# An attention kernel of two layers: a fourth score bank at times, its exponentials on VectorE

## Chip, cores, metric

One core of a Trainium2 chip. The metric is device microseconds of one execution. Quoted times are medians; a ratio is the mean time of one kernel's fast runs over the mean of the other's fast runs of the same rounds on the same chip, so it is not quite the ratio of the two medians. Intervals are 95%.

## The reference, cut

```python
def _A_ref(x, wqkv, wo):                      # 16 heads of 28, S = 2048, D = 448
    q, k, v = ...                             # from x @ wqkv
    scores = jnp.einsum("bhqd,bhkd->bhqk", q, k) * scale
    p = _softmax(scores, axis=-1)
    return merge_heads(jnp.einsum("bhqk,bhkd->bhqd", p, v)) @ wo
def _B_ref(x, w1, b1, w2, b2):                # F = 1792, squared ReLU
    ...
x = x + _A_ref(_layernorm(x), A_wqkv, A_wo)   # attention
x = x + _B_ref(_layernorm(x), B_w1, ...)      # FFN
# and both once more, with the same weights
```

## The kernel before

It is a program that plans itself. Streams of operations (scores, exponentials, attention sums, FFN chains, filler) are put in order at build time by a planner that knows a duration for each; every engine is then given its instructions in that order. The kernel divides PSUM (the memory that its matmuls write their sums to) into two score tiles of three banks each (`R_sc`), and a pool of two single banks (`R_m`) that attention outputs, FFN and QKV tiles, transposes and filler share. A bank in this text is what the code calls `bank`: a tile of 128 x 512 fp32. Filler means matmuls whose result nobody reads.

```python
R_sc, R_m, R_pt = Res(2), (Res(1), Res(1)), Res(NPT)
# scores: three units of [128, 512] per group; one unit = one head, 256 queries (or 128), so many keys
groups = [units[i:i + 3] for i in range(0, len(units), 3)]
def s_stream():
    for gi, us in enumerate(groups):
        ...                                   # 32-row matmuls, one row tile per head
        o = Op("PE", 0.22 + 0.01 * mm, fn, deps=list(deps), acq=R_sc, mode="row", sets=("s", gi), need=1 + cut)
def e_stream():                               # ScalarE: one exponential per group
    ...
    nc.scalar.activation(out=pt[:, 0:n], in_=gbuf[gi]["sc"][:, 0:n], func=AF.Exp,
                         scale=float(np.log(2.0)) * 2.0 ** -23)
# ... p_stream: sums over keys, an output bank of the pool held from the first to the last
# the filler: keeps TensorE's load up, takes a pool bank
def heat():
    for gi in range(1, len(groups)):
        yield Op("-", 0.0, None, deps=[("s", gi)])
        short = 0.74 - pl.load(WINDOW)        # planned load of the last 2.8 us
        if short <= 0 or not s_left:
            continue
        k = 1 if short < 0.14 else 2
        def junk(e):
            t = bank(o, "mt")
            for _ in range(k):
                nc.tensor.matmul(t[:, 0:D], lhsT=ident[:, :], rhs=xns[0][:, 0:D], start=True, stop=True)
        o = Op("PE", 0.19 * k, junk, deps=[("s", gi)], acq=R_m)
        ...
```

The scores come scaled by 2^23 times log2 e, so that an exponential can also be had on VectorE: add the exponent bias and convert to an integer (`take`), mask out the mantissa and the exponent field, three steps of a polynomial in the mantissa, and one that multiplies by the power of two. This code is in the kernel before (it would take the third bank of a score tile), but `LAST = 0` switches it off.

The softmax here doesn't subtract the row's maximum and nothing guards it: scores larger than these inputs give would overflow.

## Time and profile before

| | before |
|---|---|
| median of runs | 961.8 us |
| span of the profiled run | 957.4 us |
| ScalarE, TensorE, VectorE busy | 97%, 88%, 46% |
| exponentials on ScalarE | 683 (2048 units) |
| filler matmuls on TensorE | 345, 104 us |
| ScalarE's idle time before exponentials | 1.7 us |
| last exponential ends, tail after it | 936.0 us, 21.4 us |

A row of the groups gives the line, the engine, the output and inputs with shapes, the count, then busy time and mean duration, then how long the engine sat idle before these instructions and who ended that. A row of the stretches gives the busy time of TensorE, its weight loads, VectorE, ScalarE and GpSimd, then the granted TensorE clock (1.00 is full), the DMA share and GB/s. The lines of the kernel before are in the prediction.

### The profile page before, as it was taken

What the parts mean: (1) busy time and instruction counts of PE and PEld (TensorE: products, weight loads), DVE (VectorE), ACT (ScalarE), POOL (GpSimd) and SP (SyncE); (2) the same over time, 40 slices, a digit from 0 to 9 for tenths busy, and PEclk for the clock granted to TensorE, in tenths of its full rate; (3) what the DMA queues carried; (4) which work ended last, traced back from release to release, by engine and by line L of the source; (5) the groups of instructions that cost most, each with busy time, mean ns of one, the idle gap of its engine ahead of it and who ended that gap; (6) DMA issues with size and microseconds to landing.
All of it is one profiled execution on the core that took longest, in us unless ns stands there. A gap on an engine that the chain in (4) does not pass through costs nothing.

```text
span 957.4 us, 27259 instructions
## 1 busy us (share of the span) xinstructions
PE 838.9 (88%) x12123; PEld 431.9 (45%) x12123; DVE 443.1 (46%) x1151; ACT 928.7 (97%) x700; POOL 7.6 (1%) x16
## 2 busy tenths in 40 slices
PE   8999779898989898998989977779899989788886
PEld 4555334444444444444444433334444434455654
DVE  7855244555364544636464411144734434153444
ACT  6999999999999999999999999999999999999992
POOL 3000000000000000000000000000000000000000
PEclk9999999999999999999999999999999999999999
DMA  9000010000000000000000000011000000000000
GB/s 276 4 2 2 8 41 9 13 13 8 13 13 7 14 13 8 13 14 1 1 2 2 1 2 1 11 35 35 18 23 17 15 21 12 21 12 21 19 11 11
DMA packets 34467, 18.31 MB, mean 19 GB/s; under 512 B 18475, under 2 KB 33900, under 8 KB 34349
## 3 DMA queue, kind: packets, MB, share of 16 engines
q1 hardware_dynamic: 34348, 16.58, 6.2%
q8 instruction: 94, 1.54, 0.7%
q14 instruction: 25, 0.20, 0.1%
HBM read 14.26 MB, written 2.07 MB: 17 GB/s over the span
## 4 chain that ended last, share of the span: by engine, by line
ACT 76%; issue 16%; PE 6%; DVE 1%; DMA 0%; ACTq 0%
ACT pt L633 76%; PE mt L467 2%; PE sc L614 1%; PE sc L467 1%; PE mt L909 1%; PE oT L736 1%; DVE st L357 0%; DMA x_sb<-in_A_x_dram 0%; PE tp L409 0%; DVE xn L434 0%; DVE x_sb L833 0%; ACT Q_sb L482 0%; DVE tt L385 0%; DVE rstd L390 0%; DVE ve L380 0%
## 5 line engine op out<-in xcount | busy, mean ns | idle before, releaser
L633 ACT ACTIVATE pt<-sc 128x1536 bf16<-128x1536 f32 (+1 forms) x683 | 917.8, 1831 | 1.7 <-PE sc L614 1.6
L614 PE MATMUL sc<-Q_sb,K_sb 32*128 32x256 bf16 (+1 forms) x4608 | 270.5, 259 | 93.4 <-ACT pt L633 88.9
L614 PEld LDWEIGHTS <-K_sb 32*128 32x128 bf16 x4608 | 108.8, 92 | 277.5 <-issue 268.1
L736 PE MATMUL oT<-pt,V_sb 128*32 128x256 bf16 (+1 forms) x4608 | 153.8, 263 | 0.3 <-DVE K_sb L761 0.3
L467 PE MATMUL mt<-xnT,w 128*128 128x256 bf16 (+1 forms) x952 | 123.5, 266 | 6.4 <-DVE r L864 2.2
L864 DVE TENSOR_SCALAR r<-mt 128x512 bf16<-128x512 f32 (+1 forms) x109 | 74.4, 683 | 87.1 <-PE mt L467 86.6
L736 PEld LDWEIGHTS <-V_sb 128*32 128x32 bf16 x4608 | 93.0, 96 | 45.6 <-issue 41.3
L909 PE MATMUL mt<-xn,ident 128*128 128x448 bf16 x345 | 104.2, 358 | 2.4 <-DVE x_sb L833 0.7
L467 PE MATMUL mt<-w,h 128*128 128x448 bf16 x434 | 102.1, 355 | 1.5 <-DVE x_sb L833 1.2
L467 PEld LDWEIGHTS <-w 128*128 128x128 bf16 x1008 | 81.4, 99 | 43.9 <-issue 32.7
L833 DVE TENSOR_TENSOR x_sb<-x_sb,mt 128x448 bf16<-128x448 bf16 x62 | 38.2, 616 | 101.2 <-PE mt L467 101.0
L467 PEld LDWEIGHTS <-h 128*128 128x128 bf16 x448 | 34.9, 97 | 43.8 <-issue 22.3
L868 DVE TENSOR_TENSOR h<-r 128x512 bf16<-128x512 bf16 x114 | 47.7, 419 | 8.0 <-ACT r L862 4.8
L761 DVE COPY oT_sb<-oT 128x256 f32<-128x256 f32 (+1 forms) x52 | 19.7, 380 | 65.4 <-PE oT L736 64.9
L909 PEld LDWEIGHTS <-ident 128*128 128x128 bf16 x345 | 25.0, 97 | 37.8 <-issue 31.9
L357 DVE BATCH_NORM_STATS2 st<-x_sb 128x6 f32<-128x448 bf16 x64 | 39.8, 622 | 2.0 <-DMA x_sb<-in_A_x_dram 0.7
L467 PE MATMUL mt<-xnT,wk 128*128 128x256 bf16 x256 | 36.1, 276 | 2.4 <-DVE xnT L419 2.2
L822 DVE TENSOR_TENSOR oTn<-oT_sb,rec 128x256 bf16<-128x256 f32 (+1 forms) x72 | 27.7, 386 | 20.5 <-DMA rec<-scr 20.3
L467 PE MATMUL mt<-xnT,wq 128*128 128x256 bf16 x240 | 33.8, 274 | 0.6 <-DVE K_sb L488 0.5
L488 DVE CAST K_sb<-mt 128x512 bf16<-128x512 f32 x30 | 20.7, 690 | 28.3 <-PE mt L467 28.1
L763 DVE TENSOR_TENSOR K_sb<-oT,K_sb 128x256 f32<-128x256 f32 x28 | 11.9, 424 | 45.9 <-PE oT L736 45.6
L484 DVE TENSOR_SCALAR Q_sb<-mt 128x512 bf16<-128x512 f32 x30 | 20.7, 690 | 24.6 <-PE mt L467 23.4
(71 smaller groups left out, 386.6 us busy)
## 6 DMA issues: line engine op xcount, KB each, us to landing
rec<-scr SPq DMA_DIRECT2D x52, 128.0 KB
x_sb<-in_A_x_dram SPq DMA_DIRECT2D x8, 224.0 KB
out_dram<-x_sb SPq DMA_DIRECT2D x16, 112.0 KB
w<-in_B_w_dram SPq DMA_DIRECT2D x1, 1568.0 KB
w<-in_B_w_dram SPq DMA_DIRECT2D x1, 1344.0 KB
dn<-oT_sb SPq DMA_DIRECT2D x52, 4.0 KB
scr<-dn SPq DMA_DIRECT2D x52, 4.0 KB
rec<-scr SPq DMA_DIRECT2D x12, 64.0 KB
```

Of the source, the lines that this page charges most:

```text
L357: nc.vector.bn_stats(out=st[:, :], in_=x_sb[:, t0 + j, :])
L467: nc.tensor.matmul(box["t"][:, c0:c0 + n], lhsT=lhsT() if callable(lhsT) else lhsT, rhs=rhs, start=a, stop=b)
L484: nc.vector.tensor_scalar(out=dst, in0=src, scalar1=by, scalar2=None, op0=ALU.mult)
L488: nc.vector.tensor_copy(out=dst, in_=src)
L614: nc.tensor.matmul(sc[:, c0:c0 + nt * P], lhsT=K_sb[l][rows, g, (kb + i) * P:(kb + i + 1) * P], rhs=Q_sb[rows, g, t0 * P:(t0 + nt) * P], s ...
L633: nc.scalar.activation(out=pt[:, 0:n], in_=gbuf[gi]["sc"][:, 0:n], func=AF.Exp, scale=float(np.log(2.0)) * 2.0 ** -23)
L736: nc.tensor.matmul(box["t"][DHP * hh:DHP * hh + DHP, 0:n], lhsT=V_sb[l][:, kb + i, 4 * g + hh, :], rhs=p[:, c0:c0 + n], start=begin and kb ...
L822: nc.vector.tensor_tensor(out=oTn_of[l, qb][0][:, g, 0:n], in0=res["t"][:, 0:n], in1=box["r"][:, 0:n], op=ALU.mult)
L833: nc.vector.tensor_tensor(out=x_sb[:, tb, :], in0=x_sb[:, tb, :], in1=t[:, 0:D], op=ALU.add)
L864: nc.vector.tensor_scalar(out=r[:, 0:w], in0=t[:, 0:w], scalar1=0.0, scalar2=None, op0=ALU.max)
L868: nc.vector.tensor_tensor(out=h[:, 0:w], in0=r[:, 0:w], in1=r[:, 0:w], op=ALU.mult)
L909: nc.tensor.matmul(t[:, 0:D], lhsT=ident[:, :], rhs=xns[0][:, 0:D], start=True, stop=True)
```

## The change

The intent: ScalarE, the bound, gives some units to VectorE, which is idle half the time (46% busy), without shortening ScalarE's instructions. A group may get a fourth unit, whose scores go to a bank of the shared pool. Conditions are tested at each group; filler and transposes now yield the last free bank. `NEAR`, `FAR` and `LAG` were counted in groups of three units and are now counted in units, so 9 and 15 are the old 3 and 5.

```diff
-NEAR = 3
-FAR = 5
+NEAR = 9
+FAR = 15
-LAG = 5
+LAG = 6
-LAST = 0
+LAST = 690
 ...
-            if s_left and p_next[0] is not None and e_now[0] >= p_next[0] - (NEAR if n < 8 else FAR):
+            if s_left and (want[0] or p_next[0] is not None and e_now[0] >= p_next[0] - (NEAR if n < 8 else FAR)):
                 return R_m if all(r.when() is not None for r in R_m) else ()
 ...                                           # transposes of the layer norm:
-            t = Op("PE", ..., acq=pools_now(early))
+            t = Op("PE", ..., acq=pools_now(early) if early else spare(1))
 ...
+    def apart(i, now):
+        want[0] = False
+        if not LEAD <= len(gbuf) <= LAST or i + LAG > ends_at[units[i][0]]:
+            return False                       # the last six units of a pass are barred
+        if aside[0] is not None and (aside[0].end is None or aside[0].end > now):
+            return False                       # one at a time
+        if any(... keys or queries not there ...):
+            return False
+        if pl.load(SPAN, "DVE") > BUSY:
+            return False
+        near = p_next[0] is not None and e_now[0] >= p_next[0] - NEAR
+        want[0] = sum(r.when() is not None and r.when() <= now for r in R_m) < 1 + near
+        return not want[0]                     # a pool bank must be free
 ...                                           # in s_stream:
+                if at[0] < len(units) and apart(at[0], o.start):
+                    us = us + [units[at[0]]]
+                    ...
+                    dst.append(bank(x, "mt"))
+                    pl.spawn(C_PRIO, a_first(gi, x, dst[-1]))
 ...                                           # the filler:
-            o = Op("PE", 0.19 * k, junk, deps=[("s", gi)], acq=R_m)
+            o = Op("PE", 0.19 * k, junk, deps=[("s", gi)], acq=spare(1))
```

Cut: the bookkeeping by which the attention sums find the unit in the group (`where`, `done`, `got`), and the steps on VectorE, which are as before except for their source.

More of the change, by code (lines that the diff above doesn't have):

```diff
@@ L1 @@
+import itertools
 from contextlib import ExitStack
@@ L341 @@
     p_next = [None]
-    e_now = [0]
+    e_now = [0, 0]
+    want = [False]
     def engs_now(early=False):
@@ L410, in tr @@
                                             in_=xn[:, dc * P:(dc + 1) * P], identity=ident[:, :])
-            t = Op("PE", 0.07 * NDC * len(xs), tr, deps=[x[1] for x in xs], acq=pools_now(early))
+            t = Op("PE", 0.07 * NDC * len(xs), tr, deps=[x[1] for x in xs],
+                   acq=pools_now(early) if early else spare(1))
             yield t
@@ L573 @@
                 units.append((pi, kb, r, hh))
-    groups = [units[i:i + 3] for i in range(0, len(units), 3)]
-    gbuf = [{} for _ in groups]
-    ends_at = {}
-    for gi, us in enumerate(groups):
-        for pi, *_ in us:
-            ends_at[pi] = gi
-    aside = {}
-    def apart(gi):
-        us = groups[gi]
-        if len(us) < 3 or gi < LEAD or gi > LAST or gi + LAG > ends_at[us[-1][0]]:
+    ends_at = {pi: i for i, (pi, *_) in enumerate(units)}
+    gbuf = []
+    where = {}
+    at = [0]
@@ L586, in apart @@
+    aside = [None]
+    def apart(i, now):
+        want[0] = False
+        if not LEAD <= len(gbuf) <= LAST or i + LAG > ends_at[units[i][0]]:
             return False
-        if any(end is None for end in aside.values()) or pl.load(SPAN, "DVE") > BUSY:
+        if aside[0] is not None and (aside[0].end is None or aside[0].end > now):
             return False
-        aside[gi] = None
-        return True
-    def s_stream():
-        for gi, us in enumerate(groups):
-            deps = set()
-            mm = 0
-            cut = apart(gi)
-            for pi, kb, r, hh in us:
-                l, qb, g, *_ = passes[pi]
-                t0, nt = blocks[l][qb]
-                deps |= {("K", l, g, kb + i) for i in range(r)}
-                deps |= {("Q", l, g, t0 + i) for i in range(nt)}
-                mm = max(mm, r)
-            def fn(e, gi=gi, us=us):
-                sc = gbuf[gi]["sc"] = ps_sc.tile([P, 3 * 512], DT.float32, name="sc", tag="sc")
+        if any(pl.tok.get(d) is None or pl.tok[d].end + LAT["DVE"] > now for d in needs(units[i])):
+            return False
[4 more added lines that the diff above has]
+        return not want[0]
@@ new lines, in needs @@
+    def needs(unit):
+        pi, kb, r, hh = unit
+        l, qb, g, *_ = passes[pi]
+        t0, nt = blocks[l][qb]
+        return [("K", l, g, kb + i) for i in range(r)] + [("Q", l, g, t0 + i) for i in range(nt)]
+    def s_stream():
+        while at[0] < len(units):
+            gi = len(gbuf)
+            us = units[at[0]:at[0] + 3]
+            gbuf.append({"n": len(us)})
+            def fn(e, gi=gi, us=us):
+                sc = ps_sc.tile([P, 3 * 512], DT.float32, name="sc", tag="sc")
+                gbuf[gi]["sc"] = sc
+                dst = [sc[:, k * 512:k * 512 + 512] for k in range(len(us))]
+                at[0] += len(us)
+                if at[0] < len(units) and apart(at[0], o.start):
+                    us = us + [units[at[0]]]
+                    at[0] += 1
+                    x = aside[0] = gbuf[gi]["x"] = Op("PE", 0.0, None)
+                    x.res = min((r for r in R_m if r.when() is not None), key=lambda r: r.when())
+                    x.turn = len(x.res.rel)
+                    x.res.rel.append(None)
+                    dst.append(bank(x, "mt"))
+                    pl.spawn(C_PRIO, a_first(gi, x, dst[-1]))
+                for k, (pi, kb, r, hh) in enumerate(us):
+                    where.setdefault((pi, kb), []).append((gi, k, hh))
+                    if len(where[pi, kb]) == G:
+                        pl.tok["u", pi, kb] = o
@@ L612, in fn @@
                         rows = slice(DHP * hh, DHP * hh + DHP)
-                        c0 = k * 512 + i * nt * P
-                        nc.tensor.matmul(sc[:, c0:c0 + nt * P],
+                        nc.tensor.matmul(dst[k][:, i * nt * P:(i + 1) * nt * P],
                                          lhsT=K_sb[l][rows, g, (kb + i) * P:(kb + i + 1) * P],
@@ L617, in fn @@
                                          start=True, stop=True, tile_position=(DHP * hh, 0))
-            o = gbuf[gi]["s"] = Op("PE", 0.22 + 0.01 * mm, fn, deps=list(deps), acq=R_sc, mode="row",
-                                   sets=("s", gi), need=1 + cut)
-            if cut:
-                pl.spawn(C_PRIO, a_first(gi))
+            o = gbuf[gi]["s"] = Op("PE", 0.22 + 0.01 * max(u[2] for u in us), fn,
+                                   deps=list({d for u in us for d in needs(u)}), acq=R_sc, mode="row", sets=("s", gi))
             yield o
@@ L625, in e_stream @@
     def e_stream():
-        for gi, us in enumerate(groups):
+        gi = 0
+        while gi < len(gbuf) or s_left:
             yield Op("-", 0.0, None, deps=[("s", gi)])
-            n = (len(us) - (gi in aside)) * 512
+            n = gbuf[gi]["n"] * 512
             def fn(e, gi=gi, n=n):
-                e_now[0] = gi
+                e_now[:] = [e_now[0] + n // 512 + ("x" in gbuf[gi]), gi]
                 pt = gbuf[gi]["pt"] = ptp.tile([P, 3 * 512], DT.bfloat16, name="pt")
@@ L634, in fn, with a_first @@
                                      scale=float(np.log(2.0)) * 2.0 ** -23)
-            o = gbuf[gi]["e"] = Op("ACT", n / 1200 + 0.068, fn, deps=[("s", gi)], acq=R_pt, need=len(us) - (gi in aside),
+            o = gbuf[gi]["e"] = Op("ACT", n / 1200 + 0.068, fn, deps=[("s", gi)], acq=R_pt, need=n // 512,
                                    rel=gbuf[gi]["s"], sets=("e", gi))
             yield o
-    def a_first(gi):
+            gi += 1
+    def a_first(gi, x, src):
         yield Op("-", 0.0, None, deps=[("s", gi)])
@@ L644, in take @@
             box["i"] = vp.tile([P, 512], DT.int32, name="vi")
-            nc.vector.tensor_scalar(out=box["i"][:, :], in0=gbuf[gi]["sc"][:, 1024:1536], scalar1=EXP_BIAS,
+            nc.vector.tensor_scalar(out=box["i"][:, :], in0=src, scalar1=EXP_BIAS,
                                     scalar2=0.0, op0=ALU.add, op1=ALU.max)
-        c = Op("DVE", 0.70, take, acq=R_v, rel=gbuf[gi]["s"], sets=("y", gi))
+        c = Op("DVE", 0.70, take, deps=[("s", gi)], acq=R_v, rel=x)
         yield c
@@ L679, in a_rest @@
         o = Op("DVE", 0.68, close, deps=[o], acq=R_pd, rel=c, sets=("x", gi))
-        aside[gi] = gbuf[gi]["x"] = o
+        aside[0] = gbuf[gi]["x"] = o
         yield o
@@ L686, in p_stream @@
     def p_stream():
-        steps = [{} for _ in passes]
-        last_use = {}
-        for gi, us in enumerate(groups):
-            for k, (pi, kb, r, hh) in enumerate(us):
-                steps[pi].setdefault(kb, []).append((gi, k, hh))
-                last_use[gi] = pi, kb
         for pi, (l, qb, g, kbs, first, last) in enumerate(passes):
@@ L697, in p_stream @@
             r, n = 4 // nt, nt * P
-            todo = list(steps[pi].items())
+            todo = list(kbs[::r])
             end = pi == len(passes) - 1
             some = 1 if end else CHUNK
-            hold = 0 if end else max(gi for gi, _, _ in todo[min(HOLD * len(todo) // 8, len(todo) - 1)][1])
+            hold = todo[0 if end else min(HOLD * len(todo) // 8, len(todo) - 1)]
             box = {}
-            p_next[0] = hold
-            def there(parts):
-                return all(("x", gi) in pl.tok if k == 2 and gi in aside else ("e", gi) in pl.tok for gi, k, _ in parts)
@@ L707, in p_stream, with done, got @@
-            yield Op("-", 0.0, None, deps=[("e", hold)])
+            p_next[0] = next(i for i, u in enumerate(units) if u[0] == pi and u[1] == hold) + G - 1
+            def done(kb):
+                return ("u", pi, kb) in pl.tok and all(("x" if k == 3 else "e", gi) in pl.tok for gi, k, _ in where[pi, kb])
+            def got(kb):
+                yield Op("-", 0.0, None, deps=[("u", pi, kb)])
+                yield Op("-", 0.0, None, deps=[("e", gi) for gi, k, _ in where[pi, kb] if k < 3])
@@ L708, in p_stream @@
+            yield from got(hold)
             while todo:
-                now = [t for t in todo if there(t[1])][:some]
+                now = [kb for kb in todo if done(kb)][:some]
                 if len(now) < min(some, len(todo)):
-                    missing = next(t for t in todo if not there(t[1]))[1]
-                    if ("e", missing[-1][0]) not in pl.tok:
-                        yield Op("-", 0.0, None, deps=[("e", missing[-1][0])])
+                    kb = next(kb for kb in todo if not done(kb))
+                    if ("u", pi, kb) not in pl.tok or any(k < 3 and ("e", gi) not in pl.tok for gi, k, _ in where[pi, kb]):
+                        yield from got(kb)
@@ L714, in p_stream @@
                         continue
-                    if e_now[0] - missing[0][0] < NPT - KEEP and e_now[0] < len(groups) - 1 and len(todo) > len(now) + 1:
-                        yield Op("-", 0.0, None, deps=[("e", e_now[0] + 1)])
+                    if (e_now[1] - min(gi for gi, _, _ in where[pi, kb]) < NPT - KEEP and e_now[1] < len(gbuf) - 1
+                            and len(todo) > len(now) + 1):
+                        yield Op("-", 0.0, None, deps=[("e", e_now[1] + 1)])
                         continue
-                    now = [t for t in todo if there(t[1]) or t[1] is missing][:some]
@@ L720, in p_stream @@
-                    if not any(t[1] is missing for t in now):
-                        now[-1] = next(t for t in todo if t[1] is missing)
-                    yield Op("-", 0.0, None, deps=[("x", gi) for gi, k, _ in missing if k == 2 and gi in aside])
-                todo = [t for t in todo if t not in now]
+                    now = sorted(now[:some - 1] + [kb])
+                    yield Op("-", 0.0, None, deps=[("x", gi) for gi, k, _ in where[pi, kb] if k == 3])
+                todo = [kb for kb in todo if kb not in now]
@@ L724, in p_stream, with fn @@
                 begin, close = "t" not in box, not todo
-                def fn(e, now=now, begin=begin, close=close, box=box, l=l, g=g, r=r, n=n):
+                def fn(e, now=now, begin=begin, close=close, box=box, pi=pi, l=l, g=g, r=r, n=n):
                     if "t" not in box:
@@ L729, in fn @@
                         box["t"] = bank(box["o"], "oT")
-                    for kb, parts in now:
+                    for kb in now:
                         for i in range(r):
-                            for gi, k, hh in parts:
+                            for gi, k, hh in where[pi, kb]:
                                 p, c0 = gbuf[gi]["pt"], k * 512 + i * n
-                                if k == 2 and gi in aside:
+                                if k == 3:
                                     p, c0 = gbuf[gi]["pd"], i * n
@@ L738, in fn @@
                                                  rhs=p[:, c0:c0 + n],
-                                                 start=begin and kb == now[0][0] and i == 0,
-                                                 stop=close and kb == now[-1][0] and i == r - 1,
+                                                 start=begin and kb == now[0] and i == 0,
+                                                 stop=close and kb == now[-1] and i == r - 1,
                                                  tile_position=(0, DHP * hh))
-                gis = [gi for _, parts in now for gi, k, _ in parts if not (k == 2 and gi in aside)]
-                xs = [gi for _, parts in now for gi, k, _ in parts if k == 2 and gi in aside]
+                by = [(("x" if k == 3 else "e"), gi) for kb in now for gi, k, _ in where[pi, kb]]
                 o = Op("PE", 0.02 + 0.22 * len(now), fn,
-                       deps=[("e", max(hold, *gis)), *{("V", l, kb + i) for kb, _ in now for i in range(r)},
-                             *[("x", gi) for gi in xs]],
+                       deps=[*by, *{("V", l, kb + i) for kb in now for i in range(r)}],
                        acq=None if "o" in box else pools_now(),
-                       rel=[gbuf[gi]["e"] for gi in gis] + [gbuf[gi]["x"] for gi in xs], mode="col")
+                       rel=[gbuf[gi][w] for w, gi in by], mode="col")
                 box.setdefault("o", o)
@@ L896, in heat @@
     def heat():
-        for gi in range(1, len(groups)):
+        for gi in itertools.count(1):
+            if not s_left:
+                return
             yield Op("-", 0.0, None, deps=[("s", gi)])
```

## The prediction

Terms are cut from it: rules of the hardware that no trace of this case showed, and with them the price of the two masks and the four fused steps on VectorE. The sum came to 4.30 us of VectorE per unit, 4.7 with gaps between the steps. Of it only the first step, 690 ns, was a measured row; the 3.95 of the cycle and the 4.3 of the load limit come from the rest of that sum, so the count of 72 rests on the estimate. The 0.448 us per unit that ScalarE saves does not. What the trace of the kernel before shows on VectorE: 690 ns for a step of 512 columns out of PSUM, 424 ns for one on two bf16 tensors of 512 columns, 416 ns for one on two fp32 tensors of 256. The row tile is an estimate from the numbers beside it; in that trace the first three matmuls of a score group, of 32 rows each, begin within 10 ns of one another and take 278 ns each in the median.

> **What bounds the kernel now.** I read the shares of busy time first, then the chain that ended last, then the cost groups and the waits, and last the stretches of time, because what the change needs is spread unevenly over the span. From the page:
>
> ```profile
> span 957.4 us, 27259 instructions
> PE 838.9 (88%) x12123; PEld 431.9 (45%) x12123; DVE 443.1 (46%) x1151; ACT 928.7 (97%) x700; POOL 7.6 (1%) x16
> ACT 76%; issue 16%; PE 6%; DVE 1%; DMA 0%; ACTq 0%
> ```
>
> ScalarE is busy 97% of the span and carries the chain; VectorE is busy less than half. The groups by form and the waits say what ScalarE does and that nobody starves it:
>
> ```profile
> L633 ACT ACTIVATE pt<-sc 128x1536 bf16<-128x1536 f32 x682 | 916.9, 1832 | 1.7 <-PE sc L614 1.6
> ...
> L909 PE MATMUL mt<-xn,ident 128*128 128x448 bf16 x345 | 104.2, 358 | 2.4 <-DVE x_sb L833 0.7 <-DVE r L864 0.7 <-DVE xn L434 0.6
> ```
>
> ```profile
> PE sc L614 <- ACT pt L633: 88.9, 181, 0.9
> ...
> ACT pt L633 <- PE sc L614: 1.6, 3, 0.6
> ```
>
> The 2048 score units (one head, 512 scores per partition, one PSUM bank) are exponentiated three at a time. ScalarE waited 1.6 us in all for scores, TensorE 88.9 us for ScalarE to free a score tile. The mean of 1832 ns is not the pace, since neighbours overlap: 916.9/682 = 1.344 us per exponential of 1536 columns, so **0.448 us per unit**. TensorE's 88% is partly filler: the 345 matmuls with the identity (104.2 us) are junk that keeps its load up. Real work is 838.9 - 104.2 = 735 us, 77% of the span.
>
> By stretches of 24 us (columns: length, TensorE, weight loads, VectorE, ScalarE, GpSimd, clock, DMA share, GB/s):
>
> ```profile
> 72.00:96.00 24.00, 23.55 (x320) 13.05 (x320) 13.17 (x25) 24.00 (x19) 0.00 (x0) 1.00 0.01 2
> ...
> 288.00:312.00 24.00, 21.88 (x269) 10.77 (x267) 11.84 (x28) 24.00 (x20) 0.00 (x0) 1.00 0.03 8
> ...
> 576.00:600.00 24.00, 18.17 (x255) 7.39 (x251) 2.97 (x7) 24.00 (x20) 0.00 (x0) 1.00 0.00 1
> ...
> 672.00:696.00 24.00, 21.32 (x321) 12.12 (x318) 16.99 (x50) 24.00 (x19) 0.00 (x0) 1.00 0.05 13
> ```
>
> ScalarE is full in every one. VectorE runs at 0.12 to 0.71; over 96 to 936 us I got 367 us of 840, so 0.44. About 21 us at the end (the last exponential ends near 936) is a tail of the last block's FFN that this change doesn't touch.
>
> [...] A unit's contraction uses 32 rows, so three units leave one row tile empty and a fourth should nearly ride free; the trace has six such matmuls in 0.39 us where one takes 0.26, which fits.
>
> **The change, part by part.** The old form of this idea is in the kernel, switched off (its last permitted group is 0); it cut the third bank off a score tile. The new one keeps three banks for ScalarE and at times appends a fourth unit, in a pool bank, for VectorE.
>
> *Removed:* 0.448 us of ScalarE per unit moved, as 2048 units need (2048 - N)/3 exponentials. That lies on the path that sets the end.
>
> *Added on VectorE, per unit, 512 columns:* one add-and-max out of PSUM (690 ns, the row of that shape); [...] It is off the path only while VectorE has room; VectorE pays nearly ten times what ScalarE saves.
>
> *How many units, N?* The choice in the code: from group 60 (about 14 + 60 x 1.344 = 95 us) onwards; one unit at a time; VectorE's planned load of the last 12 us at most 0.9; a free pool bank; keys and queries ready; not among the last six units of a pass. With d the share of other VectorE work, a cycle is about 0.5 us for the scores and their signal, 0.3 for the operation in hand, 0.7 for the first step, 3.95/(1-d) for the rest among other work, and 0.6 of waiting for the next group start. So 2.1 + 3.95/(1-d), plus 0 to 3 us for the pool bank and the barred ends of passes (the 8-unit passes around 550 to 620 us bar three quarters of their positions). The load limit adds: at least 4.3/(0.92-d). Over VectorE's load in 12 us stretches from 84 to 936 us, scaled up 4% for a shorter kernel, this gives N = 82, 75, 69 and 64 with 0, 1, 2 and 3 us of such waiting. I take **72**, about 3.5% of all units. VectorE would then have 443 + 72 x 4.3 = 753 us of work.
>
> *Gain:* 72 x 0.448 = 32 us off ScalarE, some 24 fewer exponentials (658 left).
>
> *Given back, an estimate:* attention outputs whose last probabilities come from VectorE, FFN tiles that find one pool bank instead of two, and evictions queued behind 0.69 us steps. ScalarE's wait for scores, 1.6 us now, I put at 4 us and the tail at 1 to 2 us longer: about 5 us back. *TensorE:* 72 units of a third of 0.39 us, some 9 us less; the filler now yields the last free bank. No bound of its own: 735 of some 930 us is 79%.
>
> 961.8 - 32 + 5 = **935 us**.
>
> **The rivals.** *A, pool banks become the bound.* One pool bank holds an attention output for more than half of each pass, and FFN and QKV tiles pass through the other. A fourth score unit holds one about 1.5 us, and when it fails for want of a bank the tiles are told to wait. If that slows the FFN chains, layer 1 finds its keys late, or the tail grows. For it: VectorE spent 101 us idle waiting for FFN sums, so tiles already turn around slowly. Against it: from 552 to 624 us there is almost no FFN work, so layer 0 has some 70 us in hand, and the filler shows TensorE ahead of its work elsewhere. It would give 942 to 955 us. *B, VectorE becomes the bound in its busy stretches.* With the load held at 0.9 of planned time and real steps slower than planned[...], evictions come late, banks free late, scores come late. For it: 672 to 696 us is already at 0.71. Against it: the limit stops new units exactly there. It would cost 5 to 15 us, so 940 to 950. *C, the waiting per unit is small.* The reservation makes the next group succeed, so N is 85 to 110, and 918 to 930 us. In the quiet stretches the planner could start one every four groups, which speaks for it; the load limit at d = 0.5 and the bars in short passes speak against. *D, N is small (under 40)* as conditions rarely meet: 945 to 955 us.
>
> **Range and chances.** The bound is plainly ScalarE and the exchange rate is nearly exact; the uncertain terms are N (50 to 95, so 22 to 43 us) and what is given back (2 to 12 us). 8 in 10: 920 to 948. "Faster by over 2%" means under 942.6 us, so a net 19 us: N = 54 with 5 us lost. I give 0.77 to faster, 0.20 to within 2%, 0.03 to slower, which would need rival A at its worst.
>
> **What the profile after would show.** ScalarE still over 95% with about 658 exponentials at 1.344 us each and under 6 us of waiting for scores: the bound has not moved. Five new VectorE lines (first step, two masks, two forms of fused step) with first steps counting N[...]: the price. VectorE near 750 us. Score matmuls unchanged at 4608 but busy under 270 us: the free row tile. Fewer filler matmuls. A wait of ScalarE on scores beyond 15 us, or a gap in the layer change near 600 us, would show A or B; [...]a last exponential more than 25 us before the end would show the tail growing. I am wrong altogether if ScalarE falls under 93% busy before the tail.

## The result, and the profile after

950.5 us (948.5 to 950.8, 4 runs) against 961.9 (4 runs): ratio **0.9875** (0.9858 to 0.9892). It is faster, by 1.25% and not by the 2.8% forecast, and outside the stated range of 920 to 948. The prediction had called a time within 2% of the old one a one in five chance.

The page of the kernel after (span, busy shares, chain):

```profile
span 946.3 us, 27292 instructions
...
PE 824.6 (87%) x11997; PEld 425.4 (45%) x11997; DVE 615.3 (65%) x1483; ACT 912.5 (96%) x688; POOL 7.6 (1%) x16
...
ACT 61%; issue 18%; PE 16%; DVE 3%; DMA 2%; ACTq 0%; SPq 0%
```

ScalarE is still the bound at 96%, but its share of the chain fell from 76% to 61% and TensorE's rose from 6% to 16%. Groups by form:

```profile
L655 ACT ACTIVATE pt<-sc 128x1536 bf16<-128x1536 f32 x666 | 898.2, 1687 | 10.3 <-PE sc L637 9.7 <-ACT pt L655 0.2
...
L931 PE MATMUL mt<-xn,ident 128*128 128x448 bf16 x218 | 68.9, 377 | 6.5 <-DVE vi L668 4.0 <-DVE xn L437 1.0 <-DVE x_sb L853 0.7
L690 DVE SCALAR_TENSOR_TENSOR vh<-vh,vm 128x512 f32<-128x512 f32 x96 | 65.6, 684 | 0.8
...
L668 DVE TENSOR_SCALAR vi<-mt 128x512 int32<-128x512 f32 x48 | 33.2, 691 | 48.7 <-PE mt L637 44.8 <-PE sc L637 3.8
...
L682 DVE TENSOR_SCALAR vm<-vi 128x512 int32<-128x512 int32 x48 | 20.0, 416 | 0.5
```

The waits:

```profile
PE sc L637 <- ACT pt L655: 85.4, 166, 1.1
...
PE mt L470 <- DVE vi L668: 10.2, 22, 0.8
...
ACT pt L655 <- PE sc L637: 9.7, 19, 1.0
```

The count of first steps (L668) says that **48** units went to VectorE, not 72. Filler fell from 345 matmuls to 218. ScalarE's idle time before the exponentials grew from 1.7 to 10.3 us. In the stretches that the prediction showed:

```profile
72.00:96.00 24.00, 23.25 (x323) 12.86 (x322) 13.23 (x25) 24.00 (x20) 0.00 (x0) 1.00 0.01 2
288.00:312.00 24.00, 22.43 (x290) 12.09 (x288) 15.46 (x30) 23.64 (x18) 0.00 (x0) 0.93 0.05 13
576.00:600.00 24.00, 19.50 (x271) 9.13 (x270) 13.46 (x25) 24.00 (x20) 0.00 (x0) 1.00 0.01 2
672.00:696.00 24.00, 20.41 (x289) 10.52 (x288) 19.23 (x56) 24.00 (x20) 0.00 (x0) 1.00 0.07 19
```

VectorE's load is up in the last three, and in the second the granted clock is 0.93 and ScalarE is no longer full (23.64 of 24). That was the trail. I read the granted clock of both kernels in stretches of half a microsecond over the whole span. The kernel before has one stretch of low clock ahead of its tail (3.4 us, at 420 us); the kernel after has 13. After the first 20 us, *each* of ScalarE's waits for scores (17, from 0.17 to 0.98 us) ends inside such a stretch or within 3 us of its end, and so does the only one before. One of them closely, in stretches of 3.41 us:

```profile
322.89:326.31 3.42, 3.25 (x60) 1.71 (x62) 3.11 (x14) 3.42 (x4) 0.00 (x0) 1.00 0.07 21
326.31:329.72 3.41, 1.63 (x31) 0.77 (x32) 2.59 (x8) 3.41 (x4) 0.00 (x0) 1.00 0.00 0
329.72:333.13 3.41, 3.32 (x37) 1.49 (x36) 2.27 (x12) 2.85 (x3) 0.00 (x0) 0.50 0.00 0
333.13:336.55 3.42, 3.42 (x39) 1.57 (x33) 2.84 (x7) 3.12 (x3) 0.00 (x0) 1.00 0.02 1
```

TensorE is busy 1.63 of 3.41 us; in the next 3.41 us it runs at exactly half clock (0.50); ScalarE then loses 0.86 us. The order of events there (start, length, what; in brackets the idle time before and who ended it):

```profile
328.59 0.29 PE L637 MATMUL sc<-Q_sb,K_sb 32*128 32x256 bf16 x3 [0.95 <-ACT pt L655]
...
328.60 0.28 PE L637 MATMUL mt<-Q_sb,K_sb 32*128 32x256 bf16 x1
328.70 0.29 PE L637 MATMUL sc<-Q_sb,K_sb 32*128 32x256 bf16 x3
328.72 0.27 PE L637 MATMUL mt<-Q_sb,K_sb 32*128 32x256 bf16 x1
...
329.06 0.69 DVE L668 TENSOR_SCALAR vi<-mt 128x512 int32<-128x512 f32 x1 [0.79 <-PE mt L637]
...
329.81 0.53 PE L931 MATMUL mt<-xn,ident 128*128 128x448 bf16 x1 [0.82 <-DVE vi L668]
...
330.27 0.61 PE L637 MATMUL sc<-Q_sb,K_sb 32*128 32x256 bf16 x6
...
333.43 1.45 ACT L655 ACTIVATE pt<-sc 128x1536 bf16<-128x1536 f32 x1 [0.86 <-PE sc L637]
```

Of the 1.78 us that TensorE is idle from 326.31 to 329.72, 1.05 us are waits until ScalarE frees a score tile, with no filler in between. Then the fourth unit's scores go to the pool bank, and the filler behind them waits 0.82 us (0.74 of it in this window) for VectorE's first step to free a bank; by then the clock drops. The score group at 330.27 takes 0.61 us instead of 0.40, the filler 0.53 instead of 0.36.

The same count over all 13 stretches: in the 3.41 us ahead of each, TensorE was idle 20.3 us in sum, 15.0 of them until ScalarE freed a score tile and 3.4 for VectorE's first step, and ten of these windows hold no filler at all. In the stretches themselves TensorE was busy 52.4 of 54.6 us and waited 0.9 us for the first step: there the scores came late because TensorE worked slowly, not because it stood still. One wait of ScalarE is different. It began half a microsecond before its stretch (643.75), and TensorE had just stood 1.47 us for VectorE to empty an FFN tile:

```profile
643.00 0.60 PE L470 MATMUL mt<-xnT,w 128*128 128x256 bf16 x4 [1.47 <-DVE r L884]
...
643.53 0.44 PE L637 MATMUL sc<-Q_sb,K_sb 32*128 32x256 bf16 x6
...
644.07 2.96 ACT L655 ACTIVATE pt<-sc 128x1536 bf16<-128x1536 f32 x2 [0.85 <-PE sc L637]
```

**Where the time went.** Expected from 48 units: 48 x 0.448 = 21.5 us. Measured, from the two profiled runs: exponentials' busy time 917.8 to 899.2, so -18.6 (899.2/667 = 1.348 us each instead of 1.344, which costs 2.9); idle before them +8.6; the tail 21.4 to 19.8 us, and 0.5 us for the rest of ScalarE's work and waits. Sum: -18.6 + 8.6 - 1.6 + 0.5 = -11.1, which is the difference of the spans. Most of the 2.9 us also comes from the waits: an exponential on the heels of another added 1.343 us (median of both traces), one that began after any gap took 1.450, since it overlapped with none. The kernel before has 6 of the second kind, the changed kernel 29, so 23 x 0.107 = 2.5 us.

### The profile page after: what moved, and what is told of

Its sections match the earlier page's. It is cut to its first block, busy times and chain, and to the rows that moved or that the text cites. A ratio compares the mean times of both kernels' runs of the same rounds, so it can differ in the third digit from the quotient of the medians.

```text
span 946.3 us, 27292 instructions
## 1 busy us (share of the span) xinstructions
PE 824.6 (87%) x11997; PEld 425.4 (45%) x11997; DVE 615.3 (65%) x1483; ACT 912.5 (96%) x688; POOL 7.6 (1%) x16
## 4 chain that ended last, share of the span: by engine, by line
ACT 61%; issue 18%; PE 16%; DVE 3%; DMA 2%; ACTq 0%; SPq 0%
ACT pt L655 60%; PE mt L470 6%; PE sc L637 4%; PE oT L758 2%; DMA dn<-oT_sb 1%; PE mt L931 1%; PE sc L470 1%; DVE vi L668 1%; PE tp L411 1%; DVE st L359 0%; DMA x_sb<-in_A_x_dram 0%; DVE xn L437 0%; DVE rec L810 0%; DVE x_sb L853 0%; PE den L804 0%
## 5 line engine op out<-in xcount | busy, mean ns | idle before, releaser
L655 ACT ACTIVATE pt<-sc 128x1536 bf16<-128x1536 f32 x667 | 899.2, 1686 | 10.3 <-PE sc L637 9.7
L758 PE MATMUL oT<-pt,V_sb 128*32 128x256 bf16 (+1 forms) x4498 | 158.3, 267 | 0.0
L470 PE MATMUL mt<-xnT,w 128*128 128x256 bf16 (+1 forms) x952 | 127.1, 273 | 10.4 <-DVE vi L668 6.5
L931 PE MATMUL mt<-xn,ident 128*128 128x448 bf16 x218 | 68.9, 377 | 6.5 <-DVE vi L668 4.0
L690 DVE SCALAR_TENSOR_TENSOR vh<-vh,vm 128x512 f32<-128x512 f32 x96 | 65.6, 684 | 0.8
L668 DVE TENSOR_SCALAR vi<-mt 128x512 int32<-128x512 f32 x48 | 33.2, 691 | 48.7 <-PE mt L637 44.8
L842 DVE TENSOR_TENSOR oTn<-oT_sb,rec 128x256 bf16<-128x256 f32 (+1 forms) x72 | 27.6, 384 | 10.2 <-DMA rec<-scr 10.1
L695 DVE SCALAR_TENSOR_TENSOR pd<-vh,vi 128x512 bf16<-128x512 f32 x48 | 33.0, 687 | 0.6
```

The source lines that it names most:

```text
L470: nc.tensor.matmul(box["t"][:, c0:c0 + n], lhsT=lhsT() if callable(lhsT) else lhsT, rhs=rhs, start=a, stop=b)
L668: nc.vector.tensor_scalar(out=box["i"][:, :], in0=src, scalar1=EXP_BIAS, scalar2=0.0, op0=ALU.add, op1=ALU.max)
L690: nc.vector.scalar_tensor_tensor(out=h[:, :], in0=src, scalar=b, in1=m, op0=ALU.add, op1=ALU.mult)
L695: nc.vector.scalar_tensor_tensor(out=pd[:, :], in0=h[:, :], scalar=b0, in1=i.bitcast(DT.float32), op0=ALU.add, op1=ALU.mult)
L758: nc.tensor.matmul(box["t"][DHP * hh:DHP * hh + DHP, 0:n], lhsT=V_sb[l][:, kb + i, 4 * g + hh, :], rhs=p[:, c0:c0 + n], start=begin and kb ...
```

## The experiments

Two theories for the waits. **Clock theory:** the fourth unit and its first step take the bank that the filler used, TensorE's busy share dips, its clock is halved for a few microseconds, and scores come late. **Queue theory:** TensorE stands behind VectorE's longer queue, and the scores planned after that come late (14 us of waits on the first step are in the trace: 10.2 for FFN, QKV and projection tiles, 4.0 for filler), and the clock is a by-product. For the count there is a third question: would 72 units have brought the forecast time?

Since the plan is made at build time, each variant's count of fourth units was known before it ran. For the kernel after, every group start and the first condition it failed, in the order of the code, counted by running the kernel's planner:

```
666 group starts: 48 got a fourth unit
251 barred (59 of them the first 60 groups, 192 the last six units of a pass)
168 no pool bank free      157 the unit before not finished      42 VectorE's load
```

Summary, with "low" the stretches of low clock ahead of the tail and "idle" ScalarE's idle time before exponentials, both from the one profiled execution. They vary from one execution to the next: the profiled one was the fastest of four for the kernel after (948.5 us) and the slowest for dve_light (952.9), so a difference of a few us of idle time between two profiles can't be told from noise.

| run | units | filler | low | idle us | median us | ratio to before |
|---|---|---|---|---|---|---|
| before | 0 | 345 | 1 | 1.7 | 961.8 | |
| after | 48 | 218 | 13 | 10.3 | 950.5 | 0.9875 (0.9858 to 0.9892) |
| before_noheat | 0 | 0 | 24 | 24.9 | 989.2 | 1.0266 (1.0226 to 1.0307) |
| no4 | 0 | 349 | 5 | 3.0 | 962.9 | 1.0017 (0.9998 to 1.0036) |
| heat_rm | 38 | 325 | 4 | 5.7 | 949.9 | 0.9879 (0.9863 to 0.9894) |
| bankless | 49 | 153 + 136 | 13 | 11.1 | 949.8 | 0.9883 (0.9866 to 0.9899) |
| dve_light (wrong result) | 48 | 218 | 12 | 14.0 | 950.7 | 0.9891 (0.9869 to 0.9913) |
| fill80 | 48 | 218 + 414 | 5 | 9.5 | 947.3 | 0.9856 (0.9836 to 0.9876) |
| fill86 | 48 | 218 + 574 | 6 | 12.2 | 953.5 | 0.9926 (0.9906 to 0.9947) |
| fill60 | 48 | 218 + 140 | 9 | 9.9 | 946.6 | 0.9836 (0.9813 to 0.9860) |
| lag0 | 61 | 159 | 10 | 6.5 | 945.2 | 0.9838 (0.9822 to 0.9855) |
| best63 | 63 | 182 | 9 | 7.5 | 944.1 | 0.9817 (0.9767 to 0.9866) |
| best63_f60 | 63 | 182 + 214 | 6 | 5.0 | **937.8** | **0.9750** (0.9723 to 0.9777) |
| n70 | 70 | 162 | 13 | 27.1 | 960.3 | 0.9993 (0.9953 to 1.0034) |

The number after a plus counts filler that needs no bank; one or two filler matmuls that took a score tile at the end are left out. All of these computed the right result except dve_light.

### before_noheat: the kernel before without its filler

```diff
-    pl.spawn(9.5, heat())
```

> The kernel before with its filler matmuls (the 345 identity matmuls) left out, nothing else. Clock theory (ScalarE waits because TensorE's load dips and its clock halves for some 3.5 us): many low-clock stretches instead of two, ScalarE's wait for scores over 8 us instead of 1.6, time 968 to 990 us. Rival, queue theory (in the changed kernel scores come late because TensorE, in order, stands behind VectorE's first step on the fourth bank): the filler is harmless either way, so 959 to 963 us and waits under 3 us.

```profile
L633 ACT ACTIVATE pt<-sc 128x1536 bf16<-128x1536 f32 x682 | 922.9, 1617 | 24.9 <-PE sc L614 24.0
```

```profile
576.00:600.00 24.00, 16.44 (x207) 5.10 (x203) 2.50 (x6) 24.00 (x19) 0.00 (x0) 0.50 0.01 2
```

989.2 us, 2.7% slower, with nothing but work of no use taken away. TensorE ran at half clock for the whole of 576 to 600 us, where ScalarE stayed full because little else was to be done; elsewhere scores came late, 24.9 us in all. The clock theory's claim about this kernel is shown, and by more than I expected. The exponentials themselves also took 1.353 us each instead of 1.344: 55 of them began after a gap instead of 6, which makes 49 x 0.107 = 5.2 of the 6.0 us.

This run and the two kernels also show which busy share goes ahead of a low clock. The stretches of low clock begin on a grid of 3.413 us (in the changed kernel's trace the first and the last are 808.96 us apart, 237 steps, and all 14 lie within 0.01 us of it), and the granted clock in them is 0.50. Cutting each trace on its own grid and asking what busy share of a full-clock window went ahead of a half-clock one, up to about 907 us:

```
               windows   share of those followed by half clock              lowest shares followed by full clock
after            242     0.43 0.48 0.48 0.52 ... 0.58 0.59 0.65 (13)        0.61 0.62 0.62 0.64
before           257     0.59 (1)                                           0.62 0.65 0.65 0.66
before_noheat    183     0.25 0.39 0.39 0.40 ... 0.55 0.57 0.58 (21)        0.60 0.61 0.65 0.70
```

Of these 682 windows, every one under 0.59 busy was followed by half clock, and none over 0.65. The lower border is less sharp than that: in the changed kernel's own trace, just after the table ends, a window of 1.89 busy us in 3.41 (0.55, at 909.99) was followed by full clock. Over all fourteen traces, from 20 us to the last exponential, there are 3508 full-clock windows: all 60 under 0.55 were followed by half clock, none of the 3274 over 0.66, and those between went either way (70 half, 104 full).

### no4: the change with no fourth unit ever taken

```diff
-LAST = 690
+LAST = 0
```

> The changed kernel with the last permitted group at 0, so no fourth bank is ever taken; the other edits (filler and transposes yield the last free bank, limits counted in units) stay. Both theories: 683 exponentials, time 958 to 966 us. If the waits for scores are already 8 us here, the yielding alone cools the clock, and neither the fourth bank nor VectorE is to blame.

```profile
L655 ACT ACTIVATE pt<-sc 128x1536 bf16<-128x1536 f32 x682 | 917.4, 1770 | 3.0 <-PE sc L637 3.0
```

962.9 us, the same as before. The yielding of banks alone costs little: filler stays at 349, waits at 3.0 us, 5 low stretches. It takes the fourth unit to displace the filler.

### heat_rm: the filler may take any free bank again

```diff
-            o = Op("PE", 0.19 * k, junk, deps=[("s", gi)], acq=spare(1))
+            o = Op("PE", 0.19 * k, junk, deps=[("s", gi)], acq=R_m)
```

> The changed kernel with the filler's bank rule alone put back as it was before (it takes any free pool bank). The program now contains 38 fourth units instead of 48, so 17.0 us less for ScalarE instead of 21.5. Clock theory: low-clock stretches fall from 13 to 5 or fewer, waits under 5 us, time 946 to 950 although ten units fewer are moved. Queue theory: waits stay at 8 us or more, time 952 to 956.

```profile
L655 ACT ACTIVATE pt<-sc 128x1536 bf16<-128x1536 f32 x670 | 901.6, 1738 | 5.7 <-PE sc L637 5.6
...
L931 PE MATMUL mt<-xn,ident 128*128 128x448 bf16 x325 | 101.9, 359 | 8.7 <-DVE vi L668 2.1 <-DVE xn L437 2.0 <-DVE r L884 1.4
```

949.9 us, as fast as the changed kernel with ten units fewer (worth 4.5 us). Low stretches fell to 4, idle time to 5.7 us, a little over the 5 expected. Two things differ here, the filler's rule and the number of units, so the fall can't be put down to the filler alone. The two uses of the bank trade evenly: filler in it keeps the clock up (0.989 granted in the mean against 0.971), a fourth unit in it shortens ScalarE's work.

### bankless: filler that needs no bank, in the plan

While an attention output is open, the filler adds products with zero weights to it (`lhsT=zero, start=False`), which changes no value.

> The changed kernel with a filler that needs no bank: while an attention output is open, the filler adds products with zero weights to it (no value changes); only where none is open is it the old one. 49 fourth units, so 22.0 us less for ScalarE. Clock theory: 4 or fewer low-clock stretches before the tail, waits for scores under 4 us, time 940 to 945. Queue theory: waits near 10 us as in the changed kernel, time 949 to 952.

```profile
L658 ACT ACTIVATE pt<-sc 128x1536 bf16<-128x1536 f32 x666 | 897.8, 1681 | 11.1 <-PE sc L640 10.6
...
L938 PE MATMUL oT<-xn,zero 128*128 128x256 bf16 x110 | 18.6, 292 | 0.7 <-DVE xn L440 0.7
```

The expectation failed: 949.8 us, 13 low stretches, 11.1 us idle. The kernel did not do what I wanted, though. The filler is one stream in order, and still waited for a bank wherever no output was open; its total busy time was 49.3 + 18.6 + 2.8 = 70.7 us, against 68.9 in the changed kernel. So the run tells only that filler of another kind but the same amount changes nothing. The next ones add filler outside the plan instead.

### dve_light: the same plan, most of VectorE's work left out

`mant`, `expo` and the three polynomial steps emit nothing; `close` reads the first step's output twice. Order on all other engines is unchanged.

> Wrong result on purpose. The changed kernel, same plan, same order on every engine, but of the seven VectorE steps of each fourth unit only the first and the last are emitted: 48 x 2.9 = 139 us of VectorE work gone. Clock theory: still 12 to 14 low-clock stretches and 8 to 11 us of waiting for scores, time 947 to 951. Queue theory (VectorE's queue holds up banks and so TensorE): waits under 4 us and 940 to 944.

```profile
PE 825.2 (87%) x11997; PEld 425.8 (45%) x11997; DVE 494.1 (52%) x1243; ACT 912.7 (96%) x688; POOL 7.7 (1%) x16
```

```profile
L655 ACT ACTIVATE pt<-sc 128x1536 bf16<-128x1536 f32 x666 | 898.5, 1700 | 14.0 <-PE sc L637 13.2
```

VectorE's busy time fell from 615.3 to 494.1 us and nothing came of it: 950.7 us, 12 low stretches, 14.0 us idle (more than the 8 to 11 expected). The five steps between a fourth unit's first and last cost this kernel nothing that these runs can measure. The queue theory, as far as it rests on these steps, falls. The first step, which holds the bank, was left in; that wait belongs to the clock theory as much as to the other.

### fill80, fill86, fill60: the same plan with filler added behind score groups

```diff
+                if gi > LEAD and opened[0] is not None and pl.load(WINDOW) < 0.8:   # 0.86, 0.6
+                    t, w = opened[0]
+                    for _ in range(2 * 256 // w):
+                        nc.tensor.matmul(t[:, 0:w], lhsT=zero[:, :], rhs=wo[:, 0, 0:w], start=False, stop=False)
```

> The changed kernel, same plan with the same 48 fourth units, but with 414 filler matmuls added outside the plan that need no bank: behind a score group, where the planned load of TensorE is under 0.80 and an attention output is open, two products with zero weights are added to it. Clock theory: low-clock stretches fall from 13 to 6 or fewer, waits from 10 to under 6 us, time 942 to 947. Queue theory, or filler in TensorE's way: waits the same or longer, time 950 to 956.

> As fill80, with 574 such filler matmuls (planned load under 0.86). Clock theory: low-clock stretches 4 or fewer, waits under 5 us, time 941 to 946, unless the filler itself begins to delay scores. Queue theory: 951 to 958.

> The changed kernel, same plan with 48 units, and only 140 such zero products (planned load under 0.60). Clock theory: 5 to 9 low-clock stretches instead of 13, waits 5 to 8 us, 945 to 949; few waits outside low-clock stretches, unlike with 574 products.

```profile
L664 ACT ACTIVATE pt<-sc 128x1536 bf16<-128x1536 f32 x666 | 898.7, 1594 | 9.5 <-PE sc L641 8.7
```

```profile
PE 875.7 (92%) x12571; PEld 452.1 (48%) x12571; DVE 615.7 (65%) x1484; ACT 915.2 (96%) x688; POOL 7.6 (1%) x16
```

```profile
L664 ACT ACTIVATE pt<-sc 128x1536 bf16<-128x1536 f32 x666 | 901.0, 1554 | 12.2 <-PE sc L641 10.2
```

These runs are mixed. With 414 products low stretches fell from 13 to 5 and the time to 947.3 (expected 942 to 947), but the idle time only to 9.5 instead of under 6; 5.1 us of it sit around one long low stretch at 652 to 659 us. With 140 products: 9 stretches, 9.9 us idle (5 to 8 expected), 946.6 us. With 574: TensorE 92% busy, 953.5 us, and 14 of the 21 waits after the start now lie neither in a low stretch nor within 3 us of its end; that the filler itself is in the way of scores is the likely reason. So filler is a dose: little of it gains 3 to 4 us in the medians (the intervals of fill60 and of the changed kernel still touch), too much takes them back. That a same-plan filler removes most of the idle time is not shown.

### lag0: the bar at the end of a pass removed

```diff
-LAG = 6
+LAG = 0
```

> The changed kernel, fourth units allowed up to the end of a pass (the bar on the last six units gone): 61 units instead of 48, so 27.3 us off ScalarE instead of 21.5. If only the number of units were short: 944 to 945. Clock theory: more units mean more dips, over 13 low-clock stretches and over 11 us of waits, so at best 946 to 951. Attention sums that must wait for VectorE's late results would show as TensorE waiting for the last step.

```profile
L655 ACT ACTIVATE pt<-sc 128x1536 bf16<-128x1536 f32 x662 | 891.6, 1688 | 6.5 <-PE sc L637 6.2
```

61 units, 945.2 us: 13 more units took 5.3 us, 0.41 each, near the 0.448 of the exchange. That nearness is partly luck. In the profiled spans (946.3 to 942.4) the exponentials took 7.1 us less and the waits 3.9 less, but the tail grew from 19.8 to 27.0 us. My clock expectation (over 13 low stretches, over 11 us idle, 946 at best) was wrong here: 10 stretches, 6.5 us. The number of dips doesn't simply grow with the number of units; it depends on where the plan puts them. The expectation that only the number was short, 944 to 945, fits the time, but by this cancelling.

### n70: about as many units as predicted

```diff
-LAG = 6
+LAG = 0
-NEAR = 9
+NEAR = 0
-BUSY = 0.9
+BUSY = 1.2
```

> The changed kernel with three limits loosened so that about as many fourth units are placed as I had predicted (72): no bar at the end of a pass, no second spare bank asked for near a new attention output, VectorE's load limit off. 70 units, 31.4 us off ScalarE. If the count alone had been wrong: 940 to 943 us. If the units themselves take from TensorE's filler and from the FFN's banks (clock theory, and rival A of the prediction): 15 or more low-clock stretches, over 12 us of waits, 945 to 955 us, no better than with 61.

```profile
601.73 2.62 PE L470 MATMUL mt<-w,h 128*128 128x448 bf16 x13
...
608.39 1.03 PE L411 MATMUL tp<-ident,xn 128*128 128x128 bf16 x8 [3.30 <-DVE xn L437]
...
610.20 1.87 PE L470 MATMUL mt<-xnT,wk 128*128 128x256 bf16 x8 [0.78 <-DVE xnT L422]
...
614.21 1.45 ACT L655 ACTIVATE pt<-sc 128x1536 bf16<-128x1536 f32 x1 [10.93 <-PE mt L637]
```

960.3 us: the whole gain is gone. ScalarE waited once for **10.9 us**, at the change of layers. The lines show why: until 604 us the FFN of layer 0's last tokens runs (`mt<-w,h`), then the layer norm, transposes (608) and keys (610) follow one upon the other, and only then can the scores of layer 1 that need those keys be taken (613.5; their exponential at 614). This chain ran late, and the 70 us that the prediction had counted in hand were used up. The last of these FFN matmuls ended at 532 us in the kernel before, 566 with 48 units, 586 with 61 (lag0), 581 with 63 (best63) and 604 here. This is rival A of the prediction. The run doesn't tell how much of it is the count: it also lifts VectorE's load limit and the second spare bank near a new attention output, both of which protect this chain. Besides, 13 low stretches bring the idle time to 27.1 us.

### best63 and best63_f60: towards a better version

`LAG = 0` and `NEAR = 3` with the load limit kept (63 units); then the same plan with 214 zero products at a planned load under 0.60.

> No bar at the end of a pass and a narrower second-bank rule, VectorE's load limit kept: 63 units, 28.2 us off ScalarE. By the slope of the runs so far (38, 48 and 61 units) about 944 us; low-clock stretches 10 to 14, waits 6 to 10 us.

> best63, same plan, with 214 bank-free zero products added outside the plan where the planned load of TensorE is under 0.60. Clock theory: low-clock stretches fall to 7 or fewer, waits 3 us or more below best63, 1 to 4 us faster than best63. Filler in TensorE's way: waits outside low-clock stretches appear and it is not faster.

```profile
L655 ACT ACTIVATE pt<-sc 128x1536 bf16<-128x1536 f32 x661 | 890.3, 1725 | 7.5 <-PE sc L637 7.0 <-ACT pt L655 0.3
```

```profile
L664 ACT ACTIVATE pt<-sc 128x1536 bf16<-128x1536 f32 x661 | 890.5, 1647 | 5.0 <-PE sc L641 4.5
```

944.1 us with a wide spread (939.2 to 950.1), then **937.8** (935.9 to 940.4), 2.5% under the kernel before: the fastest version, with both remedies. Low stretches 9 and 6, idle 7.5 and 5.0; the fall of 2.5 us is less than the 3 expected, and the gain of 6 us is more than the 1 to 4; with best63 spread over 11 us its size is uncertain, though the two intervals of the ratio overlap by 0.001 only.

## Why the prediction was wrong

By its own steps:

- **The bound and the exchange rate: right.** ScalarE stayed the bound; 48 units took 16 exponentials away (683 to 667), 18.6 us of busy time where 48 x 0.448 says 21.5.
- **The price on VectorE: right.** 691 + 416 + 425 + 3 x 684 + 687 ns = 4.27 us per unit, against 4.30, of which a trace had shown only the first step beforehand. The busy time grew by less than 48 x 4.27 (to 615.3, not 648), mostly since records overlap (by 51.5 us, against 22.8 before). And dve_light shows that the five steps between first and last lay beside the path, which also answers rival B.
- **The free row tile: right, though the predicted sign did not come.** At full clock 39 score groups of four units (8 matmuls of 256 columns) took 0.400 us in the mean, 518 of three units 0.395; the one at 328.59 above is such a group. Score matmuls in all were busy 270.1 us against 270.5, no fall of a few us, since groups in half-clock stretches took longer (0.61 at 330.27).
- **The number of units: the step that failed first.** "plus 0 to 3 us for the pool bank and the barred ends of passes" gave 72. The real cycle was (926 - 95)/48 = 17.3 us, where 72 units would have been 11.5. At one group per 1.35 us, the refusals say that the bar cost 192/48 x 1.35 = 5.4 us per unit and the missing bank 168/48 x 1.35 = 4.7, so 10 us in place of at most 3. (Each start counts under the first condition that it fails; with the bar gone, in lag0, other conditions took over most of those starts and the count rose only to 61.) The bar could have been counted from the code: passes of 8, 16 and 32 units hold 448, 448 and 1152 of the 2048 units, and six barred of each make (336 + 168 + 216)/2048 = 35% of all positions. I named it only for the shortest passes. Size: 24 units x 0.448 = 10.8 us.
- **"Given back": mis-sized, and for a reason not thought of.** I put the waits for scores at 4 us, from attention sums, FFN tiles and evictions. They were 10.3, and all of those after the start but one (0.85 us, at 644) began in halved clocks or within 3 us of their end. I had read the filler as junk and its retreat as a gain for TensorE ("the filler now yields the last free bank", "No bound of its own"). It is a load that must be kept: before_noheat loses 27 us without it. Size: 6.3 us, and 2.9 more by the slower pace of exponentials, 2.5 of it the overlap lost at each wait. The sum was wrong too: of the 4 us, 1.6 were there before, so with a tail 1 to 2 us longer the text's own terms give back 3.9 us and not 5.
- **The tail: wrong sign**, 1.6 us shorter and not 1 to 2 longer. With more units it did grow, to 27.0 us in lag0.
- Together 10.8 + 6.3 + 2.9 - 3.1 + 0.5 = 17.4 us, less the 1.1 that the prediction gave back too much: 16.3, against a miss of 16 in the profiled spans and 15.5 in the medians.
- **The rivals.** D (few units) named the time, 945 to 955, but with under 40. A did not set the time of the changed kernel, which has no gap near 600 us, but it did at 70 units in n70, with two protecting limits lifted as well. Whether another plan with 72 units would have brought 935 us is not shown; the same banks and the same VectorE carry the FFN chain to the next layer, and that chain ended later with 61, 63 and 70 units than with 48.

What stays open: how much of the 8.6 us is the clock alone. All waits but one began in a dip or within 3 us of its end, and in the dips TensorE was 96% busy at half clock; the filler's role is shown in the kernel before. But filler added to the changed kernel's own plan brought back only some 3 to 4 us in time and little in the idle time of one profile.

## What to carry to other kernels

Before work is moved into a resource that an idle-time filler uses, ask what the filler is for: here a bank given to useful work cost TensorE its clock (13 stretches at half clock ahead of the tail instead of one). Count how often each of a scheduler's conditions fails, from the sizes in the code, before multiplying a gain per unit by a hoped-for number of units. And a plan that is good at 63 units can be worthless at 70, got by lifting its limits, when one chain of dependences, here at the change of layers, runs out of slack. Last, a wait costs more than its length where neighbours overlap: here 0.107 us more for each exponential that began after a gap.
